# Attention, Fourier mixing and a two-layer channel network on one core: batch 0 half by half, four staging places, low parts read early

## The chip, the core and the metric

The kernel runs on one core of a Trainium2 chip. Its time is the device time of one execution in microseconds (us); of several runs the median counts. The engines are named as the profile names them: PE (TensorE, matrix products), PEld (its weight loads), DVE (VectorE), ACT (ScalarE), POOL (GpSimd), SP (SyncE, which issues most DMAs). All five run their own instruction rows in order and wait for one another by semaphores.

## What is computed

```python
# q, k, v: (8, 8, 576, 64): batch, heads, sequence, head dimension
k_p = k.reshape(B, H, 72, 8, 64).mean(axis=3)        # keys and values pooled by 8
v_p = v.reshape(B, H, 72, 8, 64).mean(axis=3)
scores = matmul(q, k_p.T) / 8
attn = exp(scores - max); attn = attn / (sum + 1e-9)
x = (attn @ v_p) as (8, 576, 512)                    # heads side by side
u = x + real(fft(fft(x, axis=1), axis=2))            # Fourier mixing, sequence and channels
un = (u - mean) / sqrt(var + 1e-6)                   # over the 512 channels
out = u + maximum(un @ w_ch1, 0) @ w_ch2             # w_ch1 512x2048, w_ch2 2048x512
```

## The kernel before, in words

*Layout.* Activations stand with channels on the partitions: X (one batch), U (u, a ring of 1152 columns, two batches), unh and unl (the normalised u, still without the division by the standard deviation, as a rounded high part and a remainder), rb (the factor 1/std, which is multiplied in after the second product). A batch has 576 columns, a half 288.

*The front end, fe(b),* is a generator that issues the work of batch b piece by piece: loads of q, k, v; `prep_k` (sums of eight keys into kpb); `scores` for the four pairs of heads in the order 3, 2, 0, 1 (psS, maxima mx, exponentials t, sums, t times the reciprocal on POOL); `transposes` (psT, psV, psR, copied by ACT into ah and R); `values` (psX into X); then the channel transform by cosine and sine matrices (psA, psB), the sequence transform (psQ, psP), and the normalisation: sums s and U from X (lines 625 to 634), the mean by a matmul with a constant matrix (psM), X = U minus mean (L653), the cast to unh (L641), the remainder unl (L642), squares (L663) and the variance. For most pairs of heads a softmax has one wide exponential on ACT and its sums on DVE; for the pairs in `SM` ACT does ten narrow exponentials straight from psS, each with its row sum.

*The network, ffn(ro, nb, to, f0, f1),* works on nb columns and hidden slices f of 128. Per f there are 12 matmuls g (w1h with unh, w1h with unl, w1low with unh; L740), a Relu into hh on ACT (L744), the remainder hl on DVE (L745), and, one f later, 12 matmuls into four accumulators acc (L724). Batch 0 is done in four blocks of eight slices: first half f 0 to 7, second half f 0 to 7, first half f 8 to 15, second half f 8 to 15. Then come blocks of 384 columns, and the last batch in halves. When a block ends, acc is multiplied by rb and added to U on DVE (L754, L755), and two DMAs of 288 KB each write the columns (L757).

*Weights.* They arrive as 64-bit words in 34 pieces, w1 and w2 by turns, most of 128x512, 512 KB each. `load_w` (L175) loads a piece into a staging place; there are two such places, from piece 18 to 23 three (`THIRD`), and a place is loaded again when its last piece is done. Staging place k is the buffer of tag tail k. `prep_w` turns the words into floats: two ACT instructions (L193 on the words wst, L195 into wd), two DVE instructions (L198, L199), the cast to the high part w1h or w2h (L203, ACT), the remainder (L204, POOL), and a DMA of the remainder, the low part, into memory (L205). The high parts of twelve f stay on chip; `load_low` (L214) reads the low part back for every step of the network, into the seven buffers of tag w, which wd uses too.

*What sets the order.* The functions above are issued in a written order (the loop over fe0, eleven `prep_w`, the loop over fe1, then the blocks with `advance` and `need`), and a scheduler with a simulated timeline orders each engine's row from that. Where this isn't to be left to it, a block under `tc.issue_after(x)` says that its instruction stands after x; the dictionary `behind` keeps such marks:

```python
with tc.issue_after(behind["B", 0].ins) if 4 <= n < 7 else ExitStack():   # ACT's part of pieces 4 to 6
with tc.issue_after(behind["E", 0].ins) if n == 3 else ExitStack():       # DVE's part of piece 3
```

`behind["B", 0]` and `behind["E", 0]` are instructions of batch 0's channel transform. `keep_busy` puts idle matmuls (idle) into TensorE's row at named points (`BUSY`).

Of the kernel before, what the change touches and what calls it, by code (L numbers as in the profile page):

```python
# [34 lines left out]
SM = {(1, 0), (1, 2)}  # L35
# [16 lines left out]
THIRD = 18  # L52

# [30 lines left out]
def tile_kernel(ctx: ExitStack, tc: tile.TileContext, qt, kt, vm, vr, w1, w2, cad, cbd, mkd, out):  # L84
# [49 lines left out]
    pieces = [(i, f, c, w, n % (3 if THIRD <= n < 24 else 2)) for n, (i, f, c, w, _) in enumerate(pieces)] + [(1, 12, 0, 4, 1), (1, 13, 0, 4, 1)]  # L134
# [43 lines left out]
    def prep_w(n):  # L178
# [4 lines left out]
        if wide:  # L183
# [8 lines left out]
            with tc.issue_after(behind["B", 0].ins) if 4 <= n < 7 else ExitStack():  # L192
                nc.scalar.activation(hi.bitcast(F32), hi.bitcast(F32), AF.Copy, scale=REBIAS)  # L193

                nc.scalar.activation(dh[:, :, :, 0], st.bitcast(U8)[:, :, :, 3], AF.Copy, scale=1.0 / 32.0, bias=-15.5 / 32.0)  # L195

            with tc.issue_after(behind["E", 0].ins) if n == 3 else ExitStack():
# [49 lines left out]
    def fe(b):  # L247
# [271 lines left out]
        xt = wk.tile([P, S], F32, tag="k", name="xt")[0:1, 0:290]  # L519
# [105 lines left out]
        for cl in halves if b in HZ else [slice(0, S)]:  # L625
# [9 lines left out]
        yield  # L635


        def centre(cl):
            for ti in range(4):
                uh, ul = [t[:, ti, ro:ro + S][:, cl] for t in (unh, unl)]  # L640
                nc.scalar.copy(out=uh, in_=X[:, ti, cl])  # L641
                behind["z", b] = engine(ti, UL).tensor_tensor(out=ul, in0=X[:, ti, cl], in1=raw(uh), op=ALU.subtract)  # L642

        for cl in halves:
# [8 lines left out]
            nc.vector.tensor_tensor(out=X[:, :, cl], in0=Ub[:, :, cl], in1=ps.unsqueeze(1).broadcast_to([P, 4, HS]), op=ALU.subtract)  # L653
            if b in HZ:
                centre(cl)
        if b not in HZ:
            centre(slice(0, S))
# [56 lines left out]
    def ffn(ro, nb, to, f0, f1):  # L714
        cl = slice(ro, ro + nb)
        acc = [pp.tile([P, 512], F32, tag=f"acc{e}", name=f"acc{to}_{f0}_{e}")[:, 0:nb] for e in range(4)]

        def gemm2(f, hh, hl, wh, wl):
# [3 lines left out]
            for x, e in order:  # L722
                w, h = ((wh, hh), (wl, hh), (wh, hl))[x]
                nc.tensor.matmul(acc[e], lhsT=w[:, e], rhs=h, start=(f == f0 and x == 0), stop=(f == f1 - 1 and x == 2))  # L724
# [216 lines left out]
```

## Time and profile before

| | |
|---|---|
| runs | 1091.51, 1091.9, 1096.68 us; median 1091.9 |
| profiled execution | 1091.89 us, of it 1090.1 us between the first and the last recorded instruction (the span) |
| PE | 1054.2 us busy, 97% of the span |
| PEld | 1020.4 us, 94% |
| DVE | 606.5 us, 56% |
| ACT | 417.2 us, 38% |
| POOL | 252.0 us, 23% |

All times of the profile count from the start of the span. "L740" is line 740 of the kernel before; in the changed kernel most lines stand three or more further down (L193 is L196 there, L555 is L558, L641 is L645, L653 is L661, L740 is L775, L744 is L779). A group's row gives the engine, the tiles (out<-in, numbers left out), the shape, the count, and behind it busy time, mean ns of one, and idle time just before with what ended it. A row with a time at its head stands in order of time: start, duration, instruction, and in brackets the wait ahead of it. PEclk is the share of TensorE's full clock that was granted. The shares of busy time are means over a front end of some 80 us and a long stretch behind it, so they are to be read stage by stage.

### The profile page before, as it was taken

To read this page: it belongs to the slowest core of one execution; us is meant where nothing else is said; L and a number is where in the kernel's file an instruction comes from. 1 tells how busy PE (TensorE), PEld (TensorE's weight loads), DVE (VectorE), ACT (ScalarE), POOL (GpSimd) and SP (SyncE) were. 2 spreads that over 40 slices of the span, in tenths; PEclk is the share of its full clock that TensorE was granted. 3 is DMA by queue.
4 is the path that set the end of the run, shared out by engine and by line. 5 is a ranking of instruction groups with operands and counts; after the bars stand their busy time and mean duration, and the time that the engine had idled before them with its cause. 6 is when DMAs were issued, how large, how long until landed. Compare 5 with 4: busy or idle time off the path is not lost.

```text
span 1090.1 us, 17744 instructions
## 1 busy us (share of the span) xinstructions
PE 1054.2 (97%) x6626; PEld 1020.4 (94%) x6626; DVE 606.5 (56%) x1234; ACT 417.2 (38%) x1102; POOL 252.0 (23%) x262
## 2 busy tenths in 40 slices
PE   8959898999999999999999999999999999999997
PEld 7648787999999999999999999999999999999997
DVE  6596867856367355756377455756467434522112
ACT  6668764443243331444233431443324422311110
POOL 7354364211150032201140032300231101200000
PEclk9888999999999999999999999999999999999999
DMA  8479986555434454444444444445434333446563
GB/s 304 154 221 334 312 280 214 183 172 160 129 119 147 139 162 136 119 147 154 137 119 155 130 152 137 135 131 156 143 107 156 97 106 120 117 132 186 165 187 99
DMA packets 91878, 175.80 MB, mean 161 GB/s; under 512 B 10128, under 2 KB 17296, under 8 KB 91536
## 3 DMA queue, kind: packets, MB, share of 16 engines
q1 hardware_dynamic: 91504, 172.01, 50.7%
q0 software_dynamic: 288, 2.66, 0.6%
q8 instruction: 52, 0.85, 0.3%
q14 instruction: 34, 0.28, 0.1%
HBM read 156.81 MB, written 17.83 MB: 160 GB/s over the span
## 4 chain that ended last, share of the span: by engine, by line
PE 88%; DMA 4%; ACT 3%; DVE 3%; issue 1%; SPq 0%; POOL 0%; DVEq 0%; POOLq 0%
PE acc L724 36%; PE g L740 35%; PE psX L436 4%; PE psS L348 3%; DMA wst<-in_w 2%; PE psA L555 2%; PE psP L598 2%; PE psB L581 1%; PE psQ L598 1%; PE psT L389 1%; PE idle L227 1%; DVE wd L199 1%; ACT wst L193 1%; ACT wd L195 1%; PE psR L412 1%
## 5 line engine op out<-in xcount | busy, mean ns | idle before, releaser
L744 ACT ACTIVATE hh<-g 128x384 fp32r<-128x384 f32 (+1 forms) x208 | 96.5, 464 | 329.2 <-PE g L740 310.1
L745 DVE SCALAR_TENSOR_TENSOR hl<-g,hh 128x384 fp32r<-128x384 f32 (+1 forms) x208 | 108.7, 523 | 182.3 <-ACT hh L744 180.3
L724 PE MATMUL acc<-hh,w2h 128*128 128x384 f32 (+1 forms) x832 | 187.9, 329 | 0.6 <-ACT hh L744 0.6
L724 PE MATMUL acc<-hh,w2low 128*128 128x384 f32 (+1 forms) x832 | 186.9, 327 | 0.0
L740 PE MATMUL g<-unh,w1low 128*128 128x384 f32 (+1 forms) x832 | 180.6, 331 | 5.5 <-DMA w1low<-w1l 5.5
L724 PE MATMUL acc<-hl,w2h 128*128 128x384 f32 (+1 forms) x832 | 181.3, 327 | 2.0 <-DVE hl L745 2.0
L740 PE MATMUL g<-unh,w1h 128*128 128x384 f32 (+1 forms) x832 | 173.3, 328 | 8.6 <-ACT unh L641 7.4
L740 PE MATMUL g<-unl,w1h 128*128 128x384 f32 (+1 forms) x832 | 178.7, 330 | 0.0
L740 PEld LDWEIGHTS g<-unh,w1h 128*128 128x128 f32 x832 | 140.8, 191 | 9.6 <-ACT unh L641 7.5
L740 PEld LDWEIGHTS g<-unh,w1low 128*128 128x128 f32 x832 | 139.4, 190 | 9.4 <-DMA w1low<-w1l 7.3
L724 PEld LDWEIGHTS acc<-hh,w2h 128*128 128x128 f32 x832 | 143.8, 189 | 2.2 <-ACT hh L744 0.8
L724 PEld LDWEIGHTS acc<-hh,w2low 128*128 128x128 f32 x832 | 143.8, 189 | 0.1
L724 PEld LDWEIGHTS acc<-hl,w2h 128*128 128x128 f32 x832 | 141.3, 189 | 2.7 <-DVE hl L745 2.4
L740 PEld LDWEIGHTS g<-unl,w1h 128*128 128x128 f32 x832 | 140.9, 191 | 1.2 <-issue 0.4
L368 POOL TENSOR_TENSOR t<-t,sm 128x720 f32<-128x720 f32 x32 | 47.1, 1471 | 272.5 <-DVE sm L367 266.5
L283 POOL TENSOR_TENSOR k<-k 128x288 f32<-128x288 f32 (+1 forms) x56 | 38.2, 683 | 98.4 <-DMA k<-in_kt 91.4
L353 DVE TENSOR_REDUCE mx<-psS 128x6 f32<-128x432 f32 x64 | 33.1, 527 | 28.2 <-PE psS L348 27.9
L633 POOL TENSOR_TENSOR U<-X,U 128x576 f32<-128x576 f32 (+1 forms) x14 | 19.5, 1393 | 119.9 <-DVE X L617 119.9
L348 PE MATMUL psS<-kpb,q 128*128 128x144 f32 x280 | 43.3, 292 | 4.0 <-DVE t L362 4.0
L348 PEld LDWEIGHTS psS<-kpb,q 128*128 128x128 f32 x280 | 40.3, 195 | 4.3 <-DVE t L362 4.3
L754 DVE TENSOR_TENSOR acc<-acc,rb 128x384 f32<-128x384 f32 (+1 forms) x60 | 28.7, 518 | 16.4 <-PE acc L724 16.2
L365 DVE TENSOR_REDUCE sm<-t 128x10 f32<-128x720 f32 x30 | 27.0, 901 | 12.5 <-ACT t L364 12.1
(210 smaller groups left out, 1430.4 us busy)
## 6 DMA issues: line engine op xcount, KB each, us to landing
w1low<-w1l SPq DMA_DIRECT2D x208, 256.0 KB, 2.7
w2low<-w2l SPq DMA_DIRECT2D x208, 256.0 KB, 2.9
wst<-in_w SPq DMA_DIRECT2D x30, 512.0 KB, 4.6
q<-in_qt SPq DMA_DIRECT2D x28, 288.0 KB, 3.6
k<-in_kt SPq DMA_DIRECT2D x28, 288.0 KB, 3.0
v<-in_vm SPq DMA_DIRECT2D x28, 256.0 KB, 3.1
out<-U SPq DMA_DIRECT2D x18, 384.0 KB, 3.5
w1l<-wd SPq DMA_DIRECT2D x16, 256.0 KB, 4.3
```

The source lines that it names most:

```text
L283: behind["k" if n == 1 and src.shape[1] == J else "v", b] = nc.gpsimd.tensor_tensor(out=out if n == 1 else src[:, :, 0:n], in0=src[:, :, 0 ...
L348: mm = nc.tensor.matmul(ps[:, c * W2J:(c + 1) * W2J], lhsT=q[:, r0:r0 + P], rhs=kpb[g % 2], start=True, stop=True)
L353: nc.vector.tensor_reduce(out=mx[:, c0:c0 + n], in_=pv, op=ALU.max, axis=AX.X, negate=(b, g) in SM)
L365: nc.vector.tensor_reduce(out=sm, in_=t, op=ALU.add, axis=AX.X)
L368: ins = nc.gpsimd.tensor_tensor(out=t, in0=t, in1=sm.unsqueeze(3).broadcast_to([P, 5, 2, J]), op=ALU.mult)
L436: last = nc.tensor.matmul(ps, lhsT=w, rhs=a, start=(i == 0), stop=(i == len(mm) - 1))
L598: last = nc.tensor.matmul(ps, lhsT=w, rhs=a, start=(i == 0), stop=(i == 6))
L724: nc.tensor.matmul(acc[e], lhsT=w[:, e], rhs=h, start=(f == f0 and x == 0), stop=(f == f1 - 1 and x == 2))
L740: nc.tensor.matmul(ps, lhsT=w[:, c], rhs=x[:, ti, cl], start=(n == 0), stop=(n == 11))
L744: nc.scalar.activation(hh, ps, AF.Relu)
L745: nc.vector.scalar_tensor_tensor(out=hl, in0=ps, scalar=0.0, in1=raw(hh), op0=ALU.max, op1=ALU.subtract)
L754: nc.vector.tensor_tensor(out=acc[e], in0=acc[e], in1=rb[:, cl], op=ALU.mult)
```

## The change

- `SM` loses (1, 0): pair 0 of batch 1 gets the wide exponential, pair 2 keeps the ten narrow ones.
- Pieces 0 to 23 of the weights use four staging places instead of two and three. Places 2 and 3 are the buffers that the scores t of batch 0's pairs 0 and 1 have held before. Pieces 2 and 3 are loaded at a step of fe0.
- `HOLD` and `HOLDV` say behind which mark ACT's and DVE's parts of pieces 2 to 8 stand: "R" is ACT's copy of batch 0's last transposes, "B" and "E" as before, "X" is the first half of X = U minus mean.
- `EARLY`: the low parts of w1 and w2 for f = 0 are read after four pieces, those for f = 1 after six.
- Batch 0's normalisation: both halves' sums s, both psM, then the first half's U, subtraction, unh and unl, and then (behind the mark "z") the second half's U, subtraction, unh and unl. Before, sums and U of both halves came ahead of psM.
- Batch 0's small row xt moves from the tag of k into rb.
- The end of the last block: the products acc times rb go into X; each is ordered behind the one before on DVE, with the sums into U alternately on POOL and DVE, and four DMAs of 144 KB, alternately from SP's and ACT's queues. TensorE's last 12 matmuls are held in the order accumulator by accumulator.

```diff
-SM = {(1, 0), (1, 2)}
+SM = {(1, 2)}
-THIRD = 18
+HOLD = {2: "R", 3: "R", 4: "R", 5: "R", 6: "B", 7: "B", 8: "B"}
+HOLDV = {4: "E", 5: "E", 6: "X", 7: "X", 8: "X"}
+EARLY = [4, 6]
...
-    pieces = [(i, f, c, w, n % (3 if THIRD <= n < 24 else 2)) for n, (i, f, c, w, _) in enumerate(pieces)] + [(1, 12, 0, 4, 1), (1, 13, 0, 4, 1)]
+    pieces = [(i, f, c, w, n % (4 if n < 24 else 2)) for n, (i, f, c, w, _) in enumerate(pieces)] + [(1, 12, 0, 4, 1), (1, 13, 0, 4, 1)]
...
-            with tc.issue_after(behind["B", 0].ins) if 4 <= n < 7 else ExitStack():
+            with tc.issue_after(behind[HOLD[n], 0].ins) if n in HOLD else ExitStack():
...
-            with tc.issue_after(behind["E", 0].ins) if n == 3 else ExitStack():
+            with tc.issue_after(behind[HOLDV[n], 0].ins) if n in HOLDV else ExitStack():
...
-                    nc.scalar.copy(out=raw(R[0:32, a0:a1]), in_=src)
+                    behind["R", b] = nc.scalar.copy(out=raw(R[0:32, a0:a1]), in_=src)
...
-        xt = wk.tile([P, S], F32, tag="k", name="xt")[0:1, 0:290]
+        xt = (rb if b == 0 else wk.tile([P, S], F32, tag="k", name="xt"))[0:1, 0:290]
...
+        if b == 0:
+            for cl in halves:
+                sums(cl)
+            ps = [mean(cl) for cl in halves]
+            for cl, p in zip(halves, ps):
+                with tc.issue_after(behind["z", b].ins) if cl.start else ExitStack():
+                    unfold(cl)
+                less(cl, p)
+                if cl.start == 0:
+                    first = behind["X", b]
+                    behind["z", b] = centre(cl)
+                else:
+                    centre(cl)
...
+        end = to + nb == B * S and f1 == NFC
...
+        if end:
+            last = None
+            for e, q in enumerate((nc.sync, nc.scalar, nc.sync, nc.scalar)):
+                u = U[:, e, cl]
+                with tc.issue_after(last.ins) if last else ExitStack():
+                    last = nc.vector.tensor_tensor(out=X[:, e, 0:nb], in0=acc[e], in1=rb[:, cl], op=ALU.mult)
+                if e % 2:
+                    with tc.issue_after(last.ins):
+                        last = nc.vector.tensor_tensor(out=u, in0=u, in1=X[:, e, 0:nb], op=ALU.add)
+                else:
+                    nc.gpsimd.tensor_tensor(out=u, in0=u, in1=X[:, e, 0:nb], op=ALU.add)
+                q.dma_start(out[:, e, to:to + nb], u)
...
+        if n == 12:
+            load_w(2)
+            load_w(3)
...
         done_w += 1
+        if done_w in EARLY:
+            for i in range(2):
+                load_low(i, EARLY.index(done_w))
```

Here `sums` holds the s of the old loop, `unfold` its U, `mean` the psM matmul, `less` the subtraction, and `centre` the casts and remainders as before.

Three places in the engines' rows. The first is TensorE's row between batch 0's last psX (values) and its first psA (channel transform). Before:

```order
L436 MATMUL psX_1_416<-R,wlo 128x288
L227 MATMUL idle<-ident 128x128 x10
L555 MATMUL psA_0_450<-ca,f 128x258 x4
L555 MATMUL psA_1_455<-ca,f 128x258 x4
L555 MATMUL psA_2_460<-ca,f 34x258 x4
```

And now, with psS_3 the scores of batch 1's pair 3:

```order
L439 MATMUL psX_1_420<-R,wlo 128x288
L230 MATMUL idle<-ident 128x128 x10
L351 MATMUL psS_3_0_757<-kpb_76,q_3_742 128x144 x3
L351 MATMUL psS_3_3_763<-kpb_76,q_3_742 128x144 x2
L558 MATMUL psA_0_453<-ca,f 128x258 x4
L558 MATMUL psA_1_458<-ca,f 128x258 x4
L558 MATMUL psA_2_463<-ca,f 34x258 x4
```

The five score matmuls stood near psM before; now they stand ahead of psA.

The second is DVE's row behind the last sum from psP (L617, now L620), up to batch 0's unl. wd and wst are a weight piece in preparation. Before:

```order
L617 TENSOR_TENSOR U_81<-U_81,psP0_1_540 1x2
L198 TENSOR_SCALAR wd_679<-wst_667 128x512
L626 TENSOR_TENSOR s_576<-X_80 128x288
L633 TENSOR_TENSOR U_81<-X_80,U_81 128x288
L626 TENSOR_TENSOR s_576<-X_80 128x288
L633 TENSOR_TENSOR U_81<-X_80,U_81 128x288
L198 TENSOR_SCALAR wd_689<-wst_677 128x512
L633 TENSOR_TENSOR U_81<-X_80,U_81 128x288 x2
L199 SCALAR_TENSOR_TENSOR wd_679<-wst_667,wd_679 128x512
L634 TENSOR_TENSOR U_81<-X_80,U_81 128x288 x2
L199 SCALAR_TENSOR_TENSOR wd_689<-wst_677,wd_689 128x512
L634 TENSOR_TENSOR U_81<-X_80,U_81 128x288 x2
```

And now:

```order
L620 TENSOR_TENSOR U_81<-U_81,psP0_1_543 1x2
L630 TENSOR_TENSOR s_579<-X_80 128x288 x2
L638 TENSOR_TENSOR U_81<-X_80,U_81 128x288 x2
L639 TENSOR_TENSOR U_81<-X_80,U_81 128x288 x2
L661 TENSOR_TENSOR X_80<-U_81,psM0_584 128x4x288
L201 TENSOR_SCALAR wd_690<-wst_650 128x512
L201 TENSOR_SCALAR wd_700<-wst_660 128x512
L201 TENSOR_SCALAR wd_710<-wst_674 128x512
L202 SCALAR_TENSOR_TENSOR wd_690<-wst_650,wd_690 128x512
L646 TENSOR_TENSOR unl_84<-X_80,unh_83 128x288
```

Four U instead of eight and no weight piece stand ahead of the first subtraction (L661, before L653, which followed the last row shown); the other four U come behind the first half's unl.

The third is ACT's row from the weight pieces behind batch 0's channel transform on. Before:

```order
L193 ACTIVATE wst_667<-wst_667 128x512
L195 ACTIVATE wd_679<-wst_667 128x512
L193 ACTIVATE wst_677<-wst_677 128x512
L195 ACTIVATE wd_689<-wst_677 128x512
L203 CAST w1h_68<-wd_679 128x512
L203 CAST w2h_69<-wd_689 128x512
L193 ACTIVATE wst_687<-wst_687 128x512
L195 ACTIVATE wd_699<-wst_687 128x512
L641 CAST unh_83<-X_80 128x288 x4
L193 ACTIVATE wst_697<-wst_697 128x512
L195 ACTIVATE wd_709<-wst_697 128x512
L641 CAST unh_83<-X_80 128x288 x4
```

And now, with L645 the cast of the first half to unh and L779 the first Relu (hh):

```order
L196 ACTIVATE wst_684<-wst_684 128x512
L198 ACTIVATE wd_700<-wst_660 128x512
L198 ACTIVATE wd_710<-wst_674 128x512
L645 CAST unh_83<-X_80 128x288 x4
L206 CAST w1h_68<-wd_690 128x512
L206 CAST w2h_69<-wd_700 128x512
L206 CAST w1h_68<-wd_710 128x512
L196 ACTIVATE wst_698<-wst_698 128x512
L198 ACTIVATE wd_720<-wst_684 128x512
L779 ACTIVATE hh_1506<-g1_0_0_1493 128x288
L196 ACTIVATE wst_708<-wst_708 128x512
L198 ACTIVATE wd_730<-wst_698 128x512
```

Of the second half's casts none stands near the first now; a weight piece's L196 stands ahead of each of the first two Relus.

More of the change, by code (lines that the diff above doesn't have):

```diff
@@ L624, in fe, with sums @@
         s_, sh, sl = [raw(gt(2 if b in NM else 4, "s"))[:, 0:S]] + [gt(i, "s")[:, 0:S] for i in (0, 1)]
-        for cl in halves if b in HZ else [slice(0, S)]:
+        def sums(cl):
             nc.vector.tensor_tensor(out=s_[:, cl], in0=X[:, E0, cl], in1=X[:, E1, cl], op=ALU.add)
@@ L629, in fe, with unfold @@
                 nc.vector.tensor_tensor(out=sl[:, cl], in0=s_[:, cl], in1=raw(sh[:, cl]), op=ALU.subtract)
+        def unfold(cl):
             for j in range(2):
@@ L634, in fe @@
                 engine(3 - j, UE).tensor_tensor(out=o, in0=e, in1=o, op=ALU.subtract)
-        yield
         def centre(cl):
@@ L641, in centre, with mean @@
                 nc.scalar.copy(out=uh, in_=X[:, ti, cl])
-                behind["z", b] = engine(ti, UL).tensor_tensor(out=ul, in0=X[:, ti, cl], in1=raw(uh), op=ALU.subtract)
-        for cl in halves:
+                ins = engine(ti, UL).tensor_tensor(out=ul, in0=X[:, ti, cl], in1=raw(uh), op=ALU.subtract)
+            return ins
+        def mean(cl):
             ps = bank(b, f"psM{b}")[:, 0:HS]
@@ L652, in fe, with less @@
                 nc.tensor.matmul(ps, lhsT=avg, rhs=sl[:, cl], start=False, stop=True)
[L653 to L657, printed above, removed]
+            return ps
+        def less(cl, ps):
+            behind["X", b] = nc.vector.tensor_tensor(out=X[:, :, cl], in0=Ub[:, :, cl], in1=ps.unsqueeze(1).broadcast_to([P, 4, HS]), op=ALU.subtract)
+        if b == 0:
[11 more added lines that the diff above has]
+                    centre(cl)
+            behind["X", b] = first
+            yield
+        else:
+            for cl in halves if b in HZ else [slice(0, S)]:
+                sums(cl)
+                unfold(cl)
+            yield
+            for cl in halves:
+                less(cl, mean(cl))
+                if b in HZ:
+                    centre(cl)
+            if b not in HZ:
+                centre(slice(0, S))
         yield "z"
@@ L721, in gemm2 @@
                 order = [(x, e) for e in range(4) for x in range(3)]
-            for x, e in order:
+            for n, (x, e) in enumerate(order):
                 w, h = ((wh, hh), (wl, hh), (wh, hl))[x]
-                nc.tensor.matmul(acc[e], lhsT=w[:, e], rhs=h, start=(f == f0 and x == 0), stop=(f == f1 - 1 and x == 2))
+                with tc.issue_after(mm.ins) if end and f == f1 - 1 and n and x == 0 else ExitStack():
+                    mm = nc.tensor.matmul(acc[e], lhsT=w[:, e], rhs=h, start=(f == f0 and x == 0), stop=(f == f1 - 1 and x == 2))
         prev = None
@@ L751, in ffn @@
         gemm2(f1 - 1, *prev)
+        if end:
[7 more added lines that the diff above has]
+                        last = nc.vector.tensor_tensor(out=u, in0=u, in1=X[:, e, 0:nb], op=ALU.add)
+                else:
+                    nc.gpsimd.tensor_tensor(out=u, in0=u, in1=X[:, e, 0:nb], op=ALU.add)
+                q.dma_start(out[:, e, to:to + nb], u)
+            yield
+            return
         for e in range(4):
```

## The prediction

> **What bounds it now.** I read the stages first: busy time of each engine in stretches chosen by eye, then the granted clock and the DMA share.
>
> ```profile
> core 0: us, PE busy (x) PEld busy (x) DVE busy (x) ACT busy (x) POOL busy (x), PEclk, DMA share, GB/s
> 62.00:84.00 22.00, 9.67 (x39) 8.44 (x39) 19.53 (x36) 15.68 (x37) 12.58 (x12) 0.71 0.70 222
> 84.00:116.00 32.00, 31.75 (x203) 28.11 (x202) 20.67 (x41) 29.05 (x99) 13.72 (x13) 0.93 0.95 325
> 116.00:166.00 50.00, 45.49 (x290) 39.21 (x290) 39.40 (x85) 32.41 (x81) 26.68 (x22) 0.97 0.86 286
> 166.00:216.00 50.00, 45.31 (x328) 43.83 (x328) 41.62 (x94) 22.88 (x57) 20.39 (x23) 0.97 0.65 198
> 216.00:1084.00 868.00, 867.99 (x5449) 856.40 (x5447) 444.09 (x896) 278.39 (x730) 146.35 (x136) 1.00 0.46 140
> ```
>
> From 216 us on TensorE has no gap (867.99 of 868), so only what lies ahead of it and the last six microseconds can be won. The loose stretch is 62 to 84: TensorE works 9.67 of 22 us, at clock 0.71. From 84 to 116 three things are near full at once: TensorE, ScalarE (29.05 of 32) and the DMA engines (0.95). Then the waits of TensorE up to 215 us, and where they stand in time:
>
> ```profile
> PE g L740 <- ACT unh L641: 7.4, 1, 7.4
> PE g L740 <- DMA w1low<-w1l: 5.5, 6, 2.7
> PE psS L348 <- DVE t L362: 4.0, 1, 4.0
> ```
>
> ```profile
> 32.56 0.75 PE L436 MATMUL psX<-ah,wh 128*128 128x288 f32 x2 [1.90 <-ACT ah L406]
> ...
> 59.49 1.49 PE L647 MATMUL psM<-s,avg 128*128 128x288 f32 x4 [1.56 <-DVE s L626]
> ...
> 70.12 2.29 PE L740 MATMUL g<-unh,w1h 128*128 128x288 f32 x8 [7.35 <-ACT unh L641]
> ...
> 78.29 2.77 PE L348 MATMUL psS<-kpb,q 128*128 128x144 f32 x10 [3.96 <-DVE t L362]
> ...
> 81.78 1.33 PE L740 MATMUL g<-unh,w1low 128*128 128x288 f32 x4 [0.72 <-DMA w1low<-w1l]
> ```
>
> The largest wait, 7.35 us, is for the first normalised half of batch 0 (unh); the first two g products then stand until 81.78 us, since the next scores (psS) and the low parts of w1 are late.
>
> **The change, part by part.** *Batch 0 half by half.* VectorE's rows up to unh, and ScalarE's cast of it:
>
> ```profile
> 54.07 1.02 DVE L199 SCALAR_TENSOR_TENSOR wd<-wst,wd 128x512 int32<-128x512 int32 x1
> 55.02 0.74 DVE L616 TENSOR_TENSOR X<-X,psP 128x574 f32<-128x574 f32 x1
> ...
> 58.66 0.44 DVE L198 TENSOR_SCALAR wd<-wst 128x512 uint16<-128x512 uint16 x1
> 59.00 0.43 DVE L626 TENSOR_TENSOR s<-X 128x288 f32<-128x288 f32 x1
> 59.37 0.44 DVE L633 TENSOR_TENSOR U<-X,U 128x288 f32<-128x288 f32 x1
> ...
> 66.25 2.61 DVE L653 TENSOR_TENSOR X<-U,psM 128x1152 f32<-128x1152 f32 x2
> ```
>
> ```profile
> 69.66 1.41 ACT L641 CAST unh<-X 128x288 fp32r<-128x288 f32 x4
> ```
>
> From the start of L616 (55.02) to the first g product (70.12) pass 15.1 us. Afterwards the order there is: L616 to L617 (3.64 us, 55.02 to 58.66), two sums s and four half-wide U at 0.37 us from start to start (59.00 to 59.37), one half of L653 (2.61 / 2 = 1.3), one cast (1.41 / 4 = 0.35). That is 3.64 + 0.74 + 1.5 + 1.3 + 0.35 = 7.5 us, 7.6 less. The weight pieces that stood ahead of L616 (L198 and L199, to 55.02) go behind it; psP, for which it must wait, was complete at 54.16, so another 0.85:
>
> ```profile
> 44.23 1.67 PE L555 MATMUL psA<-ca,f 128*128 128x258 f32 x12
> ...
> 53.86 0.30 PE L598 MATMUL psP<-cb,AB 98*128 98x290 f32 x1
> ```
>
> *Ahead of psA.* The five score matmuls of batch 1 (psS, ten rows: 2.77 us at half clock in the row at 78.29, so 1.4 at full) move from beside psM, where TensorE waited anyway, to just before psA at 44.23, on the path. Against this, one weight preparation leaves ScalarE's row ahead of the transposes' copies (L406), and two copies of kpb (some 0.5) come in:
>
> ```profile
> 30.82 0.65 ACT L193 ACTIVATE wst<-wst 128x512 f32<-128x512 f32 x1
> 31.37 0.76 ACT L195 ACTIVATE wd<-wst 128x512 uint16<-128x512 uint8 x1
> ```
>
> Neighbours overlap by about 0.1 us (0.55 from start to start here), so the pair is 1.2, and the wait of 1.90 at 32.56 becomes 1.2. Around it the clock reads:
>
> ```profile
> 28.00:32.00 4.00, 2.59 (x19) 1.88 (x17) 0.46 (x1) 4.00 (x12) 1.53 (x2) 1.00 1.02 408
> 32.00:36.00 4.00, 3.42 (x8) 1.74 (x8) 2.24 (x5) 3.92 (x12) 0.20 (x1) 0.71 0.58 188
> 36.00:40.00 4.00, 4.00 (x8) 1.50 (x6) 1.20 (x3) 0.72 (x3) 2.01 (x2) 0.50 0.17 66
> ```
>
> A gap of 1.90 us was followed by the half clock; that of 1.56 at 59.49 was not. If it goes to half again, psS adds 1.4 to 2.8, less 0.7: first g at 70.12 - 8.45 + 0.7 to 2.1, or 62.4 to 63.8 us. If it stays full, the 7.4 us of TensorE from 32 to 40 (3.42 + 4.00) take half, less 1 us for a weight load that ScalarE is then early for: 62.4 - 3.7 + 1, or 59.7. The gap of 1.2 is nearer to the 1.56 that kept the clock; I take 60.5, a little off that end since psS may meet either, with 59.5 and 64 as ends: 9.6 us earlier than 70.12. The Trainium skill (TensorE: Matmul & The Clock Gate, Why this matters for your kernels) asks only that gaps stay under about 3 us; by that neither gap matters and g starts at 59.7, but the rows at 32 and 36 us disagree.
>
> *Four places, weights earlier, low parts early.* The first two low parts of w1 and w2 are read before g needs them, so the 0.72 at 81.78 goes. But ScalarE works its row in order, and now a weight load stands in it ahead of each of the first Relus (L193 of the eleventh piece ahead of the first). That load can be issued when VectorE has read the seventh piece (three L198 and an L199 behind L653's half, about 1.7 us), and lands as loads do:
>
> ```profile
>   DMA wst<-in_w: 13.1, 10
> ...
> DMA to landing us min/median/max: 3.5/4.6/7.9
> ```
>
> ```profile
> 83.14 0.41 ACT L744 ACTIVATE hh<-g 128x288 fp32r<-128x288 f32 x1 [0.28 <-PE g L740]
> ...
> 115.92 0.37 ACT L744 ACTIVATE hh<-g 128x288 fp32r<-128x288 f32 x1
> ```
>
> 1.4 (1.7 less the 0.35 of the cast) + 0.3 to issue + 4.6 + 1.2 (L193, L195) after g's start gives the first Relu at 68.0 (before 83.14), ends 66.9 and 71.3. From the first to the eighth Relu took 32.8 us before, with ScalarE at 29.05 of 32. The order puts more between them now: three L193, one L195 and two L203 (0.58, 0.64 and 0.51 from start to start: 3.4), four unh (1.3), four squares of twice that width (2.3, an estimate from the casts), and some 0.6 of small ones.
>
> *One softmax fewer by row groups.* Of batch 1's pair 0 ten exponentials with their read-outs go and one wide exponential comes (it counts twice here, one being the other pair's, now later):
>
> ```profile
> L360 ACT ACTIVATE t<-psS,mx 128x72 f32<-128x72 f32 x20 | 6.1, 326 | 0.8 <-DVE mx L356 0.8
> 80.08 0.79 ACT L364 ACTIVATE t<-t 128x720 f32<-128x720 f32 x1
> ```
>
> -10 x 0.305 + 2 x 0.7 = -1.65; 3.4 + 1.3 + 2.3 + 0.6 - 1.65 = 6. So ScalarE has 35.1 us between them, and 38 with the waits of before in proportion (bounds 35 and 41): eighth Relu at 106.0 against 115.9, 9.9 us ahead. VectorE takes two subtractions and a sum more, beside 20.67 of 32 busy: nothing, as even 3 us would fit.
>
> *From there on* TensorE's work is the same, and the lead stays if supply follows. DMA from 60 to 164 us was busy 90 of 104 (0.68 of 20, 0.94 of 50, 0.85 of 34):
>
> ```profile
> 60.00:80.00 20.00, 8.69 (x43) 7.82 (x42) 17.87 (x33) 14.13 (x32) 11.02 (x10) 0.78 0.68 220
> 80.00:130.00 50.00, 47.14 (x290) 41.74 (x288) 37.07 (x79) 41.05 (x128) 21.77 (x19) 0.88 0.94 327
> 130.00:164.00 34.00, 31.66 (x200) 26.64 (x201) 24.95 (x49) 21.22 (x53) 20.51 (x18) 1.00 0.85 272
> ```
>
> About 2.4 MB (four low parts, a piece, k and q of batch 1) move ahead of 60, 7 us at 327 GB/s; 83 in 94 us is no fuller than before. I keep the lead; ends: 5 us lost, or 9.2 won (TensorE's gaps of 4.5 and 4.7 in 116 to 216).
>
> *xt in rb* frees k for the earlier load; its cost is nil, as POOL idles before it. k's sums of batch 1 (some 1.5 us) come between POOL's multiplications of t; TensorE came to those t later than POOL was done, so I take nothing, and at most 1 us of the front's upper end.
>
> *The end.* Now four products, then four sums, two issues of 288 KB:
>
> ```profile
> 1083.63 1.56 DVE L754 TENSOR_TENSOR acc<-acc,rb 128x288 f32<-128x288 f32 x4 [1.86 <-PE acc L724]
> 1085.10 1.53 DVE L755 TENSOR_TENSOR U<-U,acc 128x288 f32<-128x288 f32 x4
> 1085.93 1.12 SPq L757 DMA_DIRECT2D out<-U  x2
> ```
>
> With each acc finished in turn, the first product starts near 1082.75, and mult, mult, add, mult, mult, add on VectorE at 0.38 ends near 1085.1, POOL's second sum (0.8, an estimate) too; the last issue falls near 1085.2 instead of 1086.5, with half the bytes. 1.5 us, ends 1.0 and 2.0. The Trainium skill (DMA: Bandwidth & Descriptors, Issuing engines are not separate DMA queues) grants the second queue only the issue time: by the row 0.56 us of these.
>
> **Sum.** 9.9 + 1.5 = 11.4 off the profiled execution of 1091.89 us (span 1090.1, and 1.8 around it), which is the median of the runs shown (1091.9): 1080.5.
>
> **Rivals.** *Clock stays up and loads come fast:* g at 59.7, first Relu 6.4 us later (a load of 3.5), half of the 9.2 us of later gaps closed: 17 to 19 off, 1074. For it: the shorter gap; against: full DMA from 84. The Trainium skill (TensorE: Matmul & The Clock Gate, What's actually happening) has the clock set over a free-running window, so that the phase alone may choose between this and the sum.
> *The lead is given back:* ScalarE and DMA already were at 0.91 and 0.95 from 84 to 116, and later waits for w1low grow (5.5 us before). Only the end and some 2 us stay: 1088.4.
> *Slower:* each of the ten L193 between the first and eighth Relu waits for its load, and TensorE behind the Relu. It decides at 1.14 us each (11.4 lost); at 1.7 the time is 1097.5. L193 waited 13.1 / 10 = 1.3 us where it waited at all; four places should thin that out.
> *Nothing happens* can't be: the order changes ahead of the largest wait.
>
> **Numbers.** About 0.5% (5.5 us) is what a measurement can tell from no change. Chances: the sum 0.57 (its own range 1077 to 1086), clock and loads 0.23, given back 0.16, slower 0.04. So faster 0.80, same 0.16, slower 0.04. The range 1073 to 1087.5 leaves out the worse half of the given-back case, the slower one, and the best ends of the first rival.
>
> **What would show it.** First g near 60 with a wait under 2 us; first Relu near 68 and eighth near 106; clock at 32 to 44 us; no wait on w1low before 84; TensorE without gaps from about 205; and the last out issue 1.3 us sooner after the last matmul. Wrong, if L193 waits ahead of unh or the Relus for over 1 us each, or psA starts after 46.

## The result, and the profile after

The changed kernel takes 1086.2 us (median of nine runs, 1083.9 to 1088.5), the kernel before, beside it, 1092.0 us (nine runs): ratio 0.9947, 95% interval 0.9927 to 0.9967. That is 5.8 us less, where 11.4 had been forecast. The time lies inside the range (1073 to 1087.5), near its upper end and just above the likeliest case's own range (1077 to 1086). The profiled execution took 1087.56 us with a span of 1085.6, 4.5 less than the span before; the working below goes by that pair. The medians given below for unl_first and low_fewer_held include one run far off each (3605.7 and 1286.1 us), without which they are 1085.9 and 1085.8; the ratios leave it out.

The stages, with the same columns as before (busy time of PE, PEld, DVE, ACT, POOL, then clock, DMA share and GB/s):

```profile
62.00:84.00 22.00, 16.50 (x92) 14.82 (x92) 21.92 (x39) 14.82 (x36) 8.45 (x6) 0.84 0.69 212
84.00:116.00 32.00, 27.89 (x178) 23.09 (x177) 24.85 (x43) 28.32 (x81) 17.87 (x14) 1.00 0.94 326
116.00:166.00 50.00, 43.75 (x279) 37.18 (x278) 39.04 (x84) 31.40 (x78) 25.21 (x22) 0.97 0.74 250
166.00:216.00 50.00, 46.22 (x344) 44.16 (x343) 42.49 (x101) 21.92 (x56) 20.11 (x23) 1.00 0.69 211
216.00:1084.00 868.00, 864.43 (x5422) 852.85 (x5420) 444.39 (x891) 277.86 (x729) 147.49 (x138) 1.00 0.46 140
```

From 62 to 84 us TensorE works 6.8 us more than before, at a higher clock. From 84 to 116 it works 3.9 us less (178 matmuls instead of 203), though the two kernels have the same products to do: there most of the lead goes. VectorE is busy 21.92 of 22 us from 62 to 84 (19.53 before). From 216 us to its last product TensorE has no gap, as before.

TensorE's largest waits for batch 0's normalisation and its weights, up to 300 us, and the rows in which the first g products stand:

```profile
PE g L775 <- DMA w1low<-w1l: 4.6, 5, 1.5
PE g L775 <- DVE unl L646: 3.0, 2, 1.5
PE g L775 <- DVE hl L780: 2.3, 2, 1.9
PE g L775 <- ACT unh L645: 0.7, 1, 0.7
```

```profile
63.95 1.53 PE L775 MATMUL g<-unh,w1h 128*128 128x288 f32 x8 [0.74 <-ACT unh L645]
65.47 0.53 PE L775 MATMUL g<-unl,w1h 128*128 128x288 f32 x2
67.51 0.53 PE L775 MATMUL g<-unl,w1h 128*128 128x288 f32 x2 [1.50 <-DVE unl L646]
69.56 1.09 PE L775 MATMUL g<-unl,w1h 128*128 128x288 f32 x3 [1.52 <-DVE unl L646]
```

The wait for unh fell from 7.4 to 0.7 us, and the first g starts at 63.95 instead of 70.12. But the remainder unl is late next: TensorE waits for it twice, 1.5 us each. ScalarE's rows of the first and eighth Relu, and of the first Relu of the first block of 384 columns (before: 83.14, 115.92 and 242.75):

```profile
72.29 0.38 ACT L779 ACTIVATE hh<-g 128x288 fp32r<-128x288 f32 x1
...
112.76 0.41 ACT L779 ACTIVATE hh<-g 128x288 fp32r<-128x288 f32 x1
...
239.17 0.49 ACT L779 ACTIVATE hh<-g 128x384 fp32r<-128x384 f32 x1 [0.86 <-PE g L775]
```

So the lead is 10.9 us at the first Relu, 3.2 at the eighth and 3.6 at 240 us.

Two things of the new order show in single rows. VectorE and POOL around the second unl:

```profile
65.83 1.31 POOL L207 TENSOR_TENSOR wd<-wd,w1h 128x512 f32<-128x512 f32 x1 [13.35 <-ACT w1h L206]
65.94 1.52 DVE L646 TENSOR_TENSOR unl<-X,unh 128x288 fp32r<-128x288 f32 x1
...
67.10 1.48 POOL L207 TENSOR_TENSOR wd<-wd,w2h 128x512 f32<-128x512 f32 x1
67.38 1.76 DVE L202 SCALAR_TENSOR_TENSOR wd<-wst,wd 128x512 int32<-128x512 int32 x1
```

An unl that takes 0.45 us alone took 1.52, and a piece's second instruction 1.76 instead of 0.68, each begun 0.1 and 0.3 us behind a subtraction on POOL and ended 0.3 and 0.6 us behind its end. And SP's queue, with the DMA engines beside it:

```profile
52.51 0.32 SPq L208 DMA_DIRECT2D w2l<-wd  x1
65.11 4.43 SPq L178 DMA_DIRECT2D wst<-in_w  x3
```

```profile
56.00:62.00 6.00, 4.36 (x33) 3.95 (x32) 5.93 (x16) 2.10 (x3) 0.00 (x0) 1.00 0.25 97
```

The eleventh piece's load needs the place of the seventh, whose part on VectorE now stands behind the first X minus mean. SP waits for it 12.3 us, and the DMA engines are busy 0.25 of the time from 56 to 62 us, where it was 0.91.

The end, with the last of TensorE's rows:

```profile
1079.83 0.81 POOL L798 TENSOR_TENSOR U<-U,X 128x288 f32<-128x288 f32 x1 [140.18 <-DVE X L793]
...
1080.14 0.30 PE L759 MATMUL acc<-hl,w2h 128*128 128x288 f32 x1
1080.18 0.77 DVE L796 TENSOR_TENSOR U<-U,X 128x288 f32<-128x288 f32 x1
...
1081.39 0.79 POOL L798 TENSOR_TENSOR U<-U,X 128x288 f32<-128x288 f32 x1 [0.76 <-DVE X L793]
1081.71 0.78 DVE L796 TENSOR_TENSOR U<-U,X 128x288 f32<-128x288 f32 x1
```

From TensorE's end to the span's end pass 5.16 us (1080.44 to 1085.6); before, 6.11 (1083.30 + 0.69 to 1090.1). The end brought 0.95 us.

### The profile page after: what moved, and what is told of

Same layout as the page of the kernel before. It is cut to its first block, busy times and chain, and to the rows that moved or that the text cites. A ratio compares the mean times of both kernels' runs of the same rounds, so it can differ in the third digit from the quotient of the medians.

```text
span 1085.6 us, 17737 instructions
## 1 busy us (share of the span) xinstructions
PE 1051.1 (97%) x6626; PEld 1016.3 (94%) x6626; DVE 615.3 (57%) x1233; ACT 414.0 (38%) x1083; POOL 256.0 (24%) x264
## 4 chain that ended last, share of the span: by engine, by line
PE 86%; DVE 5%; ACT 3%; DMA 3%; POOL 1%; issue 1%; SPq 0%; DVEq 0%; POOLq 0%; ACTq 0%
PE g L775 35%; PE acc L759 35%; PE psX L439 3%; PE psS L351 3%; PE psA L558 2%; PE psP L601 2%; PE psB L584 1%; PE psQ L601 1%; PE psT L392 1%; DMA w2l<-wd 1%; POOL wd L207 1%; DMA w1low<-w1l 1%; ACT wd L198 1%; DMA k<-in_kt 1%; PE psR L415 1%
## 5 line engine op out<-in xcount | busy, mean ns | idle before, releaser
L779 ACT ACTIVATE hh<-g 128x384 fp32r<-128x384 f32 (+1 forms) x208 | 96.6, 464 | 338.1 <-PE g L775 318.4
L775 PE MATMUL g<-unh,w1low 128*128 128x384 f32 (+1 forms) x832 | 181.1, 331 | 4.6 <-DMA w1low<-w1l 4.6
L775 PE MATMUL g<-unl,w1h 128*128 128x384 f32 (+1 forms) x832 | 178.2, 328 | 3.0 <-DVE unl L646 3.0
L775 PE MATMUL g<-unh,w1h 128*128 128x384 f32 (+1 forms) x832 | 172.4, 326 | 3.1 <-DVE hl L780 2.3
L775 PEld LDWEIGHTS g<-unh,w1low 128*128 128x128 f32 x832 | 140.1, 190 | 7.8 <-DMA w1low<-w1l 5.9
L775 PEld LDWEIGHTS g<-unh,w1h 128*128 128x128 f32 x832 | 139.7, 189 | 4.6 <-DVE hl L780 2.8
L775 PEld LDWEIGHTS g<-unl,w1h 128*128 128x128 f32 x832 | 139.9, 189 | 4.3 <-DVE unl L646 3.7
```

Of the source, the lines that this page charges most:

```text
L775: nc.tensor.matmul(ps, lhsT=w[:, c], rhs=x[:, ti, cl], start=(n == 0), stop=(n == 11))
L779: nc.scalar.activation(hh, ps, AF.Relu)
```

## The experiments

All are edits of the changed kernel, timed beside the kernel before. A ratio is to the kernel before, so 0.9947 is "like the change"; its interval of some 0.2% to either side means that a difference of under 2 us can't be told from none. The time of a single row, such as the eighth Relu, is that of one profiled execution. Where an edit adds lines, the same instruction stands a few lines further down in its rows (L778 there is the changed kernel's L775).

**Edits that left the order to the scheduler.** *dve_free:* pieces 6 to 8 without their mark on VectorE.

```diff
-HOLDV = {4: "E", 5: "E", 6: "X", 7: "X", 8: "X"}
+HOLDV = {4: "E", 5: "E"}
```

> VectorE's part of weight pieces 6 to 8 no longer stands behind the first half of X = U minus mean. Supply theory (the lead of batch 0 is given back because weights arrive too late: the places of pieces 6 to 8 stay full until 64 to 69 us, SP issues nothing from 52.9 to 65.1 us, and the DMA engines are at 0.25 from 56 to 62): SP issues loads again before 58, the DMA share from 56 to 66 rises above 0.6, first g up to 3 us later than 63.95, but the eighth Relu 2 to 5 us ahead of 112.8, time 1081 to 1085. ScalarE theory (its row, 28.3 us busy of 32 from 84 to 116, sets the Relus): the hole closes too, but the eighth Relu is at 112.8 or later by what first g is later, time 1086 to 1089.

1099.2 us, ratio 1.0059 (1.0038 to 1.0079). The DMA share from 56 to 66 us rose from 0.16 to 0.53, but the scheduler put five pieces ahead of the first X minus mean (6 to 8 and two more), the first g came at 72.26 (psM waited 7.8 us for s) and the eighth Relu at 116.7. Neither theory foresaw it.

*lock_off:* the subtraction of pieces 6 to 8 on VectorE.

```diff
-        nc.gpsimd.tensor_tensor(out=d0, in0=d0, in1=raw(wh), op=ALU.subtract)
+        if n in (6, 7, 8):
+            with tc.issue_after(behind["z", 0].ins):
+                nc.vector.tensor_tensor(out=d0, in0=d0, in1=raw(wh), op=ALU.subtract)
+        else:
+            nc.gpsimd.tensor_tensor(out=d0, in0=d0, in1=raw(wh), op=ALU.subtract)
```

> The subtraction for the low parts of pieces 6 to 8 is done on VectorE behind batch 0's first unl, instead of on POOL between them. Port theory (an unl of 1.07 us more and a piece's instruction of 1.08 us more, both beside a POOL subtraction): the two take 0.37 and 0.6 us, the fourth unl ends near 67.3 instead of 69.4, first Relu near 70 instead of 72.3. If these two were slow for another reason: they stay near 1.45 and 1.7 us. As to the end: by the supply theory the eighth Relu stays within 1 us of 112.8 and the time within 1 us of 1086.2; if what leads the Relus is the front path alone, 2 us less.

1102.3 us, 1.0086 (1.0068 to 1.0105). Every unl took 0.45 us or less and every second instruction of a piece there 0.68, and the first Relu followed 5.9 us behind the first g (65.78) instead of 8.3: the port theory holds (VectorE was slow because of POOL's subtraction beside it). The end was 16 us later than the change's, which nothing in those rows explains: the eighth Relu was 2.8 us behind the change's (115.56) and the first Relu of the first block of 384 columns 4.2 us (243.33), so most of the loss falls later still.

*low_reads_fewer* and *act_less* are given with their held forms below; free, they took 1104.3 us (1.0102, 1.0081 to 1.0122) and 1091.9 us (0.9993, 0.9977 to 1.0008).

> Leaves out the reads of the low parts of w1 and w2 for seven of the first sixteen steps, which work with those of the step before instead: 14 reads of 256 KB less, 3.7 MB or 11 us of DMA at 327 GB/s, and no wait for those low parts. Supply theory: the lead is kept or grows, eighth Relu at 104 to 108, time 1077 to 1082. ScalarE theory: eighth Relu at 111 to 113, time 1085 to 1087.

> Leaves out ScalarE's first instruction of weight pieces 9 to 20 (12 of 0.58 us, 7 us, eight or nine of them ahead of the eighth Relu), so that those weights have other values; nothing else is taken away. ScalarE theory: the eighth Relu 4 to 5 us ahead of 112.8, time 1081 to 1083. Supply theory: under 2 us ahead, since each piece saves 0.6 us of its own chain only, time 1084.5 to 1086.5.

Less work, and up to 18 us more time: the edits had shifted the scheduler's simulated times, and with them the order of all that follows. In the traces the rows of TensorE, VectorE and ScalarE of these four runs are in another order than the change's, in far more places than the edits name. In low_reads_fewer the eighth Relu came at 109.31, near the supply theory's 104 to 108; the sixteenth, at 177.59, is 17.1 us behind that of the same omission with the order held (160.46). TensorE in three stretches of low_reads_fewer, and then of the held one:

```profile
116.00:216.00 100.00, 89.39 (x577) 79.32 (x577) 69.89 (x149) 50.62 (x133) 43.73 (x46) 0.91 0.62 194
216.00:300.00 84.00, 81.14 (x519) 79.19 (x519) 46.04 (x113) 30.86 (x95) 12.63 (x14) 0.98 0.50 154
300.00:1076.00 776.00, 773.29 (x4797) 759.75 (x4796) 403.64 (x800) 248.57 (x641) 134.11 (x123) 1.00 0.46 137
```

```profile
116.00:216.00 100.00, 91.09 (x621) 82.03 (x620) 81.13 (x181) 52.88 (x132) 43.99 (x45) 0.97 0.66 206
216.00:300.00 84.00, 84.00 (x544) 82.25 (x543) 41.30 (x94) 28.13 (x86) 14.75 (x18) 1.00 0.50 149
300.00:1076.00 776.00, 776.00 (x4850) 766.50 (x4849) 396.48 (x790) 249.10 (x642) 131.61 (x119) 1.00 0.46 139
```

By 216 us the held one has done 44 matmuls more in the last hundred, and it has no gap behind; the free one still has gaps of 2.9 and 2.7 us there.

**Edits with every engine's row held.** In the other eight an order edge from each instruction to its predecessor in the changed kernel's row held all five rows, so that only what the edit names differs. The traces bear this out: TensorE's row has the change's order, product for product, in all eight (with the idle matmuls more in idle_fill), and the other engines' rows differ only where the edit says so. The changed kernel with the edges alone was not run; five of the held edits end within 1 us of its 1086.2.

*unl_first:*

```diff
 VectorE's row:  X minus mean, L201 x3, 
-                L202, unl, L202, unl, L202, unl, unl
+                unl, unl, unl, unl, L202, L202, L202
```

> All engines' rows held as in the changed kernel, and only VectorE's second instruction of pieces 6, 7 and 8 moved behind the first half's four unl (before, one stood ahead of each of the first three). Port theory (the second unl took 1.52 us and the third piece's instruction 1.76, each beside a POOL subtraction that the piece before it released): with the pieces behind, POOL is idle during the unl, they take 0.37 us each, the first g is complete near 68.5 and the first Relu starts near 69 instead of 72.3. Rival (they were slow for another reason): the unl still take over 1 us. As to the end, supply theory (weights arrive too late from 84 us on): eighth Relu within 1 us of 112.8 and the time within 1 us of 1086.2. Front-path theory (what the first g gains stays): 2.5 to 3 us less, 1083.5.

1087.0 us, 0.9957 (0.9941 to 0.9973). Four unl in the time of one:

```profile
65.61 1.55 DVE L646 TENSOR_TENSOR unl<-X,unh 128x288 fp32r<-128x288 f32 x4
...
71.64 0.68 ACT L196 ACTIVATE wst<-wst 128x512 f32<-128x512 f32 x1 [1.96 <-DMA wst<-in_w]
...
73.27 1.09 PE L759 MATMUL acc<-hh,w2h 128*128 128x288 f32 x3 [4.42 <-ACT hh L779]
```

The port theory holds again. But the first Relu started at 72.85 all the same: ahead of it in ScalarE's row stands the eleventh piece, whose load has not landed. The first g was 1.25 us later in this execution (65.20), so the Relu followed it by 7.65 us instead of 8.34. The eighth came at 112.56, as supply expected.

*act_less_held:* ScalarE's first instruction of pieces 9 to 20 (L196) left out; VectorE's L202 does an AND instead of an OR for those pieces, at the same place.

```diff
-                nc.scalar.activation(hi.bitcast(F32), hi.bitcast(F32), AF.Copy, scale=REBIAS)
+                if not 9 <= n <= 20:
+                    nc.scalar.activation(hi.bitcast(F32), hi.bitcast(F32), AF.Copy, scale=REBIAS)
```

> All engines' rows held as in the changed kernel; left out is ScalarE's first instruction of weight pieces 9 to 20 (12 of 0.58 us, eight or nine of them ahead of the eighth Relu), so that those weights have other values. ScalarE theory (its row, busy 28.3 of 32 us from 84 to 116, sets the Relus): eighth Relu 4 to 5 us ahead of 112.8, time 1081 to 1083. Supply theory: under 2 us ahead, time 1084.5 to 1086.5.

1086.3 us, 0.9948 (0.9934 to 0.9961); eighth Relu at 112.09. ScalarE is not the bound by itself: some 5 us less of its work gave 0.7 at the eighth Relu.

*low_fewer_held:*

```diff
     def load_low(i, n):
+        if n in (3, 5, 7, 9, 11, 13, 15):
+            lows[i, n] = lows[i, n - 1]
+            return
```

> All engines' rows held as in the changed kernel; left out are the reads of the low parts of w1 and w2 in seven of the first sixteen steps, which use those of the step before instead: 14 reads of 256 KB, 3.7 MB or 11 us of DMA at 327 GB/s, and the waits for them. Supply theory: eighth Relu at 107 to 110 instead of 112.8, TensorE's waits for w1low under 2 us, time 1080 to 1083.5. ScalarE theory: eighth Relu at 111 to 113, time 1085 to 1087.

1086.0 us, 0.9939 (0.9923 to 0.9956); eighth Relu at 111.36. Both lie where the ScalarE theory had them, which act_less_held doesn't bear out. TensorE's waits for w1low fell from 4.6 to 1.7 us, as the supply theory had it, but others took their place:

```profile
86.48 0.80 PE L762 MATMUL acc<-hl,w2h 128*128 128x288 f32 x4 [2.21 <-DVE hl L783]
```

*pool_less_held:* POOL's subtractions of pieces 6 to 20 left out.

```diff
-        nc.gpsimd.tensor_tensor(out=d0, in0=d0, in1=raw(wh), op=ALU.subtract)
+        if not 6 <= n <= 20:
+            nc.gpsimd.tensor_tensor(out=d0, in0=d0, in1=raw(wh), op=ALU.subtract)
```

> All engines' rows held as in the changed kernel; left out are POOL's subtractions for the low parts of pieces 6 to 20 (15 of 1.3 us), so that those low parts have other values. Port theory (VectorE's instructions of two inputs that took 0.9 to 1.1 us more stood beside them, 3.3 us from 62 to 84 and 4.7 from 84 to 116): this excess falls under 1 and under 2 us. By the port as the bound: eighth Relu 4 to 6 us ahead of 112.8, time 1080 to 1082. By full stages, of which VectorE is one of three: 1 to 2.5 us ahead, time 1083.5 to 1085.5.

1085.9 us, 0.9942 (0.992 to 0.9965). What VectorE's instructions took above their shortest (those with over 0.3 us more) fell from 3.3 to 0 us between 62 and 84, and from 5.5 to 3.0 between 84 and 116. In this execution the first g came late, at 67.04 (the granted clock was 0.63 and 0.51 from 52 to 54 and 54 to 56 us, 1.00 in the change); the eighth Relu followed it by 45.9 us instead of 48.8, at 112.98, where neither theory had it. So the port is not the bound alone; what it costs in time isn't shown by this run.

*all_less_held:* the three omissions together.

> All engines' rows held as in the changed kernel, with the three omissions together: ScalarE's first instruction of pieces 9 to 20, the low parts' reads of seven steps, POOL's subtractions of pieces 6 to 20. Theory of full stages (each alone gave at most 1.7 us, since the next one takes its place): together more than their sum, eighth Relu 7 to 12 us ahead of 112.8, time 1074 to 1079. Rival (the rows' order itself holds TensorE: batch 1's scores, transposes and values stand between its products at fixed places and wait for a chain of their own): about the sum or less, eighth Relu 2 to 4 us ahead, time 1081 to 1084.

1081.8 us, 0.9911 (0.9888 to 0.9933); eighth Relu at 108.69. That is 4.1 us ahead where the three alone gave 0.7, 1.4 and -0.2, but not the 7 to 12 of the theory of full stages; by the time the rival is right, and by the Relu it misses its range (2 to 4) by 0.1.

```profile
62.00:84.00 22.00, 15.44 (x101) 13.44 (x100) 21.10 (x46) 14.38 (x38) 0.33 (x1) 0.99 0.75 226
84.00:116.00 32.00, 30.18 (x196) 26.52 (x196) 23.07 (x44) 26.29 (x80) 6.84 (x6) 0.96 0.89 310
```

Even so relieved, VectorE is busy 21.1 of 22 us from 62 to 84, and TensorE, with 30.2 of 32 from 84 to 116, has little left to win there.

*whole_held:* on VectorE, the second half's four U put back ahead of the first subtraction; the rest of the half-by-half order stays.

```diff
 VectorE's row:  s, s, 
-                U x4 (first half), X minus mean, ..., unl, U x4 (second half)
+                U x8, X minus mean, ..., unl
```

> All engines' rows held as in the changed kernel, and only batch 0's halves undone on VectorE: the four U of the second half (0.37 us each, 1.5 us) stand ahead of the first half's subtraction again. First g at 65.4 instead of 63.95. Front-path theory (the prediction's: what the first g gains or loses stays): eighth Relu near 114.3, time 1087.7. Theory of full stages (from 62 us on VectorE, ScalarE and the DMA engines are each so near full that the front's lead is lost whatever it is): eighth Relu within 0.7 us of 112.8, time within 1 us of 1086.2.

1085.8 us, 0.9955 (0.9937 to 0.9973); first g at 64.15, eighth Relu at 111.50. The four U cost what was expected, between psM and the first g:

```profile
59.10 1.24 PE L652 MATMUL psM<-s,avg 128*128 128x288 f32 x4 [1.64 <-DVE s L630]
64.15 2.00 PE L774 MATMUL g<-unh,w1h 128*128 128x288 f32 x8 [2.02 <-ACT unh L645]
```

That is 5.05 us against 3.76 (60.19 to 63.95), but psM was 1.1 us earlier in this execution, for a reason that the part on the first g below gives, and at the end nothing is left of either (the eighth Relu even came 1.3 us sooner, which neither theory had): the place of these four U by itself is worth nothing that can be measured.

*idle_fill:* 22 idle matmuls ahead of the transposition that waits for rt.

```diff
+            if b == 0 and gi:
+                keep_busy(22)
             nc.tensor.transpose(out=ps[0:32, 2 * P:3 * P], in_=rt[:, 4], identity=ident)
```

> All engines' rows held as in the changed kernel, and 22 idle matmuls (2.5 us) put into TensorE's row where it waits 2.64 us for rt (29.6 to 32.3 us). Clock theory (that gap is followed by half the clock from 38 to 44 us, and the prediction's miss on the first g comes from it): the clock stays at 1.0 until 44, psA starts 2.5 to 4 us earlier than 46.4, first g at 60 to 61.5 instead of 63.95. Rival (the half clock comes from something else): 0.5 from 38 to 44 again, first g at 63.95 or up to 0.3 later. As to the end: supply theory, the time within 1.5 us of 1086.2; front-path theory, 3 us less.

1090.4 us, 0.9992 (0.9974 to 1.0009): slower than the change. The clock did stay at 1.00 from 20 to 48 us, and psA began at 43.90, 2.2 us sooner than in the change. But VectorE's split of the odd channels (f, which psB needs) came no sooner (49.58 against 49.32), and then the half clock came where the change had the full one:

```profile
50.00:56.00 6.00, 5.63 (x25) 4.66 (x26) 3.24 (x8) 4.68 (x12) 2.71 (x2) 0.50 0.96 306
```

psP's last product ended at 59.71 instead of 57.21, and the first g came those 2.5 us later, at 66.45. The eighth Relu came at 120.72, after a 2.6 us wait for w1low:

```profile
109.51 0.80 PE L777 MATMUL g<-unh,w1low 128*128 128x288 f32 x4 [2.59 <-DMA w1low<-w1l]
```

The profiled execution is the slowest of its twelve (1098.6; the others 1086.6 to 1092.3), so its rows overstate the loss.

*f_first:* pieces 4 and 5 behind the odd channels' split.

```diff
 VectorE's row:  f (even), xe, 
-                L201, L201, L202, L202 (pieces 4, 5), f (odd), A, A
+                f (odd), L201, L201, L202, L202 (pieces 4, 5), A, A
```

> All engines' rows held as in the changed kernel, and only VectorE's four instructions of pieces 4 and 5 (46.7 to 49.4 us) moved behind the split of the odd channels (f, 49.32), which psB waits for. Theory (VectorE's row, not TensorE's clock, sets the path there: with full clock from 36 to 44 us, as two of the runs had it, the first g came no sooner): psB's wait for f is under 0.3 us and the first g at 62 to 63.2 instead of 63.95. Rival (the clock sets it): first g at 63.95 or later where the clock is 0.5 up to 44, near 60 where it is 1.0. As to the end: within 1.5 us of 1086.2 by full stages.

1088.8 us, 0.9979 (0.9963 to 0.9995): slower than the change, though the two intervals just touch, and the first g later, at 65.71. The odd split came at 47.20, 2.1 us sooner, as soon as psA had read the even channels. psB no longer waits for f, but for A, which the same pieces now stand ahead of:

```profile
50.67 0.89 PE L584 MATMUL psB<-ca,f 128*32 128x256 f32 x6 [1.42 <-DVE A L538]
```

Even so psB's last product ended at 51.56, 0.5 us sooner than in the change. Behind it, with the granted clock at 0.69 from 52 to 54 us and 0.50 from 54 to 56 (1.00 in the change), 2.3 us were lost: psP's last product ended at 58.96 instead of 57.21, 1.75 later, and the first g is later by as much. By its words the rival came true (the clock was 0.50 from 36 to 42 us), but not for its reason, and what makes the whole kernel slower stays open.

## Why the prediction was right in sign and half in size

The sum said 11.4 us; the profiled pair differs by 4.5 in the span. Term by term: first g 60.5, measured 63.95 (3.45 lost); from it to the first Relu 7.5, measured 8.34 (0.84 lost); from the first to the eighth Relu 38, measured 40.47 (2.47 lost); from there on the lead was to stay, and grew by 0.4; the end 1.5, measured 0.95 (0.55 lost). 11.4 - 3.45 - 0.84 - 2.47 + 0.4 - 0.55 = 4.5.

**First g: the clock, and an engine that was left out.** The prediction set it by TensorE's clock between 32 and 44 us: 59.7 at full, 62.4 to 63.8 at half, and chose 60.5 because a gap of 1.2 us seemed short enough. That gap all but went, and another of 2.64 us came at 32.27 (psV now waits for rt, a copy of ScalarE's). The clock fell to half from about 38 to 45 us, and psA began at 46.14, which the prediction had named as a sign of being wrong (after 46). But with the full clock the first g would have gained only a part of it, since VectorE's row reaches the same place at the same time:

```profile
46.14 1.69 PE L558 MATMUL psA<-ca,f 128*128 128x258 f32 x12
```

```profile
48.11 1.27 DVE L202 SCALAR_TENSOR_TENSOR wd<-wst,wd 128x512 int32<-128x512 int32 x2
49.32 0.76 DVE L512 TENSOR_TENSOR f<-tmpO,f 128x576 fp32r<-128x576 f32 x1
```

The split of the odd channels (L512) stands behind four instructions of pieces 4 and 5, which end at 49.38 with the two L202; it also needs that psA has read the even channels (before, it waited 2.49 us for that, in f_first 2.18), which is done at 49.22. whole_held has the change's rows up to psM, and met the full clock from 36 to 64 us:

```profile
43.74 1.69 PE L558 MATMUL psA<-ca,f 128*128 128x258 f32 x12 [1.38 <-ACT f L511]
...
49.24 1.91 PE L584 MATMUL psB<-ca,f 128*128 128x256 f32 x14 [1.22 <-DVE f L512]
```

```profile
48.45 0.74 DVE L512 TENSOR_TENSOR f<-tmpO,f 128x576 fp32r<-128x576 f32 x1
```

psA begins 2.4 us sooner there and has read the even channels at 46.80, but the odd split comes only at 48.45, and psM 1.1 us sooner than in the change (59.10 against 60.19). act_less_held and all_less_held, also at 1.00 from 36 to 64, have psM at 60.38 and 60.15. So of the 3.45 us the half clock cost at most 1.1; in whole_held 1.65 go to VectorE's row, and the rest is not traced. VectorE is busy without a gap there: two of its instructions ahead of the splits took 1.73 and 1.81 us beside POOL instead of 0.75 and 0.87, then come the four of pieces 4 and 5. The prediction followed the pieces that leave the row ahead of L616 and not those that enter it ahead of psB. Where the half clock fell behind the odd split, more was lost: in idle_fill and f_first some 2.2 us each up to the last psP.

On the clock itself: of two gaps of the same length at this place, the one of 3.23 us in low_fewer_held was followed by full clock up to 48 us, and the one of 3.22 us in unl_first by the half clock from 32 to 36. After the one of 2.64 us in the change the half clock came only at 38, and after the one of 2.63 us in act_less_held within 1 us or so (0.57 from 32 to 36). So a gap's length doesn't tell, as the prediction took it to. The free-running window of the Trainium skill (TensorE: Matmul & The Clock Gate, What's actually happening), by which the phase decides, agrees with these rows.

**First Relu: two locks at once.** The prediction had ScalarE wait for the eleventh piece. In the change the first g itself was late, by unl behind POOL's subtractions; with that away (unl_first) the eleventh piece was what the Relu waited for, and it gained 0.7 us. The same lock can fall the other way: in whole_held and act_less_held POOL's subtraction was held up (3.04 and 3.77 us instead of 1.31), every unl took 0.46 us or less, and the first Relu followed the first g by 6.0 and 6.2 us, in whole_held behind a wait of 1.02 us for the eleventh piece's load. So the predicted wait was real, and in the change it was covered. At the eighth Relu nothing of these 2 us is left (111.50 in whole_held, 111.36 in low_fewer_held, where the unl were slow).

**First to eighth Relu: not a sum of ScalarE's work.** The term was ScalarE's 35.1 us with waits in proportion. act_less_held shows that 5 us of that work are worth 0.7: the term's reasoning was wrong, and its size came near by chance. What was missed is that VectorE, called free here ("even 3 us would fit" in 84 to 116), had its new work in 62 to 84, where it is full.

ScalarE, the low parts' reads and POOL's subtractions, taken away one at a time, gave 0.7, 1.4 and -0.2 us at the eighth Relu and no measurable time; together 4.1, and 1081.8. That looks like more than the sum, but these are single executions: whole_held, in which no work is left out, has its eighth Relu 1.3 us ahead too. At the first Relu of the first block of 384 columns (239.17 in the change) the three are 1.4, 1.7 and 1.4 us ahead (237.81, 237.49, 237.75) and together 5.0 (234.15), so there they all but add up, as the rival had it. That limits cover one another is therefore not shown. Even with all three away the stretch from the first to the eighth Relu took 39.3 us, more than the 38 of the sum. That the rows hold TensorE there, since the products, batch 1's front end and the weights are interleaved at fixed places, would fit this, but no run changed that order alone.

**The end** was mis-sized by the same lock between VectorE and POOL: VectorE's two sums took 0.77 and 0.78 us instead of 0.38, each beside POOL's sum. That is 0.8 us, more than the 0.55 that the end lost.

So the likeliest case had the sign and the places of the gain, and the time is inside the range; but the rival "the lead is given back" (1088.4) is nearer in time and names what happened: 10.9 us of lead at the first Relu, 3.2 at the eighth. The slower rival, loads ahead of the Relus at 1.7 us each, did not come: in the change's profile none of these L196 waits for its load, and such waits show only in other executions of the same order (1.96 us in unl_first, 1.02 and 1.76 in whole_held).

**What stays open.** Which part of the change brings the 3.6 us that stay: not the place of the four U (whole_held). The rest of the half-by-half order, the four places, the marks, the early low parts and the softmax's form were not undone one by one. The hole in SP's loads from 53 to 65 us was not filled in a held order either, so its price isn't known; dve_free changed too much else to tell. And since free edits with less work ended up to 18 us later, part of the 5.8 us may lie in the order that the scheduler happened to find for the changed kernel.

## What to carry to other kernels

Where a scheduler orders the rows by a simulated time, an edit's effect is its own and that of a new order everywhere behind it; here the second reached 18 us, three times the change's whole gain. To learn what one step is worth, hold the rows and change only that step, and read more than one execution before a row's time is put down to the edit: with the rows held, the first g was up to 2.5 us later where the granted clock fell at another place. And in a stage in which VectorE, ScalarE and the DMA engines are each near full, a lead should not be carried through in a sum unchanged: here 10.9 us at the first Relu were 3.2 at the eighth. Ask what is late next at each fixed place of the bounding engine's row.

## What the runs showed of the hardware

Instructions of VectorE with two operands on chip took longer while a POOL subtraction ran: 1.52 us instead of 0.45, 1.76 instead of 0.68, 0.77 instead of 0.38. In lock_off and unl_first, where POOL was idle beside them, the first two were back at the short values. In whole_held and act_less_held it was the other way round: unl stayed short, and the POOL subtraction took 3.04 and 3.77 us instead of 1.31. The Trainium skill (SBUF — State Buffer, Who interferes with whom) has a VectorE instruction with two inputs in SBUF contend with a POOL instruction that reads there, calls this an exclusive lock, and lets the order of issue decide who waits. The rows agree with the lock. As to the order they don't tell: POOL's subtraction began 0.11 us ahead of the second unl in the change and 0.12 us ahead of it in whole_held, and VectorE waited in the one, POOL in the other.
